# A page of output weights in two transfers, and a gate and an output sum put in another order, in a two-layer decode kernel on Trainium2

## The chip, the cores and the metric

The kernel runs on one core of a Trainium2 chip. The engines are named as in the profile: PE (TensorE, matrix products; PEld is its weight load), DVE (VectorE), ACT (ScalarE), POOL (GpSimd) and SP (SyncE, which here issues nearly all transfers). A core has 16 DMA engines. The metric is the device time of one execution in microseconds (us), as the median of several executions. The profile comes from one further execution.

## The reference

One token goes through two identical layers, each an attention over a cached window and then a gated feed-forward block. The caches and the weights are the same in both layers.

```python
def _A_ref(x, k_cache, v_cache, wq, wo):
    # x: (1, 1, 640); 32 heads of 192; window W = 4096 of 32768 cached positions
    q = (x @ wq).reshape(1, 1, 32, 192) ...
    k = k_cache[:, :, Sk - W:, :]
    v = v_cache[:, :, Sk - W:, :]
    scores = einsum("bhqd,bhkd->bhqk", q, k) * (192 ** -0.5)
    o = einsum("bhqk,bhkd->bhqd", softmax(scores), v)
    return o.reshape(1, 1, 6144) @ wo

def _B_ref(x, w1, w3, w2):            # 640 -> 1536 -> 640
    return (silu(x @ w1) * (x @ w3)) @ w2

x = A_x
x = x + _A_ref(_layernorm(x), ...)
x = x + _B_ref(_layernorm(x), ...)
x = x + _A_ref(_layernorm(x), ...)
x = x + _B_ref(_layernorm(x), ...)
```

All inputs are bf16. Some 1.5 MB for each head's K window, as much for its V window, 7.9 MB each for wq and wo and 5.9 MB for w1, w2 and w3 make the work one of moving data: every weight meets a single vector.

## The kernel before

**Pages and the queue.** SBUF holds an arena of 16 slots of 12,288 bytes per partition. A list, `loads`, names every page in the order in which it is wanted: for each layer five pages of wq, the K and V windows head by head (V trails K by six heads), six pages of wo, and four of the feed-forward block. These four are `fa` (most of w1), `fb` (most of w3), `fc` (the rest of w1, the rest of w3 and four of the twelve row chunks of w2, three transfers) and `fd` (five more chunks of w2). The last three chunks of w2 stay in SBUF in `keep` from layer 0, and the last three chunks of wo in `wo5`. `refill` (line 200) issues transfers from SP as long as a slot is free; `done` frees a slot and calls `refill`. So the order of transfers is fixed by the list, and their time by free slots. There is one further limit: the framework gives the transfers eight completion semaphores in turn, so that a transfer is issued only when the one eight places ahead has landed. Fourteen heads' K pages (`RETAIN`) are kept from layer 0 and not loaded again in layer 1.

A transfer covers all 128 partitions. Each of the 16 DMA engines moves eight of the rows and reports on its own, and a transfer counts as landed when all 16 have.

**The end of a layer.** Everything that the change touches lies behind the last V page, most of it in the last 20 us.

- `wo_proj` (line 397) multiplies the 48 chunks of the attention's output with wo, page by page in the order 0 to 5. Page 4 (`("o", 1, 4)`, nine chunks, one transfer of 1440 KB in layer 1) is the last that arrives; page 5 is `wo5`. Each chunk is two matmuls of 128x320, spread over four column groups of PE.
- `y_to_residual` (line 245) copies the sums to SBUF on ACT (L247) and DVE (L248), turns them with five small matmuls, and adds them to the residual `xsq` (L252).
- `layernorm` (line 229) squares (L230), sums over partitions with one fp32 matmul, and works out the mean and the scale on DVE and ACT (L234 to L242). It writes `xs`.
- `ffn` (line 417) multiplies `xs` with the pages: g with `fa`, u with `fb`, then the last quarter-rows of g and u with `fc`. g is copied out by ACT (L444), u by DVE (L445). Three small matmuls each turn g and u into the partition layout, both into the same bank `m_ps`. Then come exp(-g) on ACT (L451), a copy of u (L454), g*u (L456), 1+exp (L458), its reciprocal (L459) and the product (L460), which gives `htd`, the twelve columns of the block's hidden vector.
- In layer 0, `y_open` (line 390) zeroes two PSUM tiles with two matmuls and 24 matmuls multiply `htd` with w2.
- In layer 1, `last_rows` (line 477) forms the output. At the start of `ffn`, POOL has spread the residual x over a matrix `xw` and built an identity in a free slot (L422 to L429). `last_rows` adds x through five fp32 matmuls with `xw` (ten instructions, as fp32 goes in two passes), then the 48 matmuls of w2's chunks in the order 0 to 3, 9 to 11, 4 to 8. Chunk 8 is the last transfer of the kernel, 160 KB. DVE copies the row (L489) and SP sends it out (L491).

PE, DVE and ACT each run their instructions in the program's order.

Of the kernel before, what the change touches and what calls it, by code (L numbers as in the profile page):

```python
# [15 lines left out]
P = 128  # L16
D = 640
NCH = 5
# [29 lines left out]
def kernel(  # L48
# [79 lines left out]
    ptm = cst.tile([P, 16 * PW], BF16, name="ptm")  # L128
    otd = cst.tile([P, 48], BF16, name="otd")
    htd = cst.tile([P, 12], BF16, name="htd")  # L130
    zero = cst.tile([P, 32], BF16, name="zero")
    nc.gpsimd.memset(zero[:], 0.0)
    w20 = cst.tile([P, 768], BF16, name="w20")
    qt_sb = cst.tile([P, H, 6], BF16, name="qt_sb")
# [28 lines left out]
    for layer in range(2):  # L163
        for c in range(NCH):
            loads.append((("q", layer, c), [(0, PGW, wq_v[c])]))
        for i in range(H + LEAD):
            for kind, g, cache in (("v", i - LEAD, A_v_cache), ("k", i, A_k_cache)):
                if not 0 <= g < H:
                    continue
                h = head(layer, g)  # L170
                if kind == "k" and layer == 1 and h in RETAIN:
                    if h == STASH:
                        loads.append((("k", 1, h), []))
                    continue
                loads.append(((kind, layer, h),
                              [(0, PGW, cache[0, h, S0:SK, :].rearrange("(p t) d -> p (t d)", p=P))]))
        for w in range(6):
            parts = []
            for at, ci in enumerate(wo_order(layer)[9 * w:9 * w + 9]):
                blk, e = ORDER[layer][ci // 12], ci % 12  # L180
                if parts and parts[-1][2] == blk and parts[-1][3] + parts[-1][1] == e:
                    parts[-1][1] += 1
                else:
                    parts.append([at, 1, blk, e])
            parts = [(640 * at, 640 * n, wo_v[blk][:, 640 * e:640 * (e + n)]) for at, n, blk, e in parts]
            if w < 5:
                loads.append((("o", layer, w), parts))
            elif layer == 0:
                assert len(parts) == 1 and parts[0][1] == 1920
                loads.append((None, [(wo5[:], parts[0][2])]))  # L190
        loads.append((("fa", layer), [(0, PGW, w1_v[:, 0:PGW])]))
        loads.append((("fb", layer), [(0, PGW, w3_v[:, 0:PGW])]))
        loads.append((("fc", layer), [(0, 1536, w1_v[:, PGW:]), (1536, 1536, w3_v[:, PGW:]),
                                      (3072, 2560, w2_v[:, 0:2560])]))
        fd = [(0, 3200)] if layer == 0 else [(0, 1280), (1280, 1280), (2560, 640)]
        loads.append((("fd", layer), [(o, n, w2_v[:, 2560 + o:2560 + o + n]) for o, n in fd]))
        if layer == 0:
            loads.append((None, [(keep[:], w2_v[:, 5760:7680])]))
# [197 lines left out]

    def wo_proj(layer):
        y_ps = y_open("y_ps")
        for w in range(6):
            pg = page(("o", layer, w)) if w < 5 else wo5  # L400
            for cc, ci in enumerate(wo_order(layer)[9 * w:9 * w + 9]):
                n = 9 * w + cc
                j = n % 4
                for nh in range(2):
                    mm(y_ps[nh][32 * j:32 * j + 1, 0:320], lhsT=otd[:, ci:ci + 1],
                       rhs=pg[:, 640 * cc + 320 * nh:640 * cc + 320 * nh + 320],
                       start=False, stop=(n >= 44), tile_position=(0, 32 * j))
            if w < 5:
                done(("o", layer, w))
        y_to_residual(y_ps)  # L410
# [6 lines left out]
    def ffn(layer):  # L417
        if layer == 1:
            assert not loads
            spare = free[0] * PGW  # L420
            ident = arena[:, spare:spare + 64].bitcast(F32)
            nc.gpsimd.memset(ident, 0.0)  # L422
            for j in range(4):
                nc.gpsimd.affine_select(out=ident, in_=ident, compare_op=ALU.not_equal, fill=1.0, base=-32 * j,
                                        pattern=[[-1, 32]], channel_multiplier=1)
            xw = arena[:, spare + 64:spare + 64 + 1280].bitcast(F32)
            nc.gpsimd.memset(xw, 0.0)
            for j in range(4):
                nc.gpsimd.tensor_copy(out=xw[32 * j:32 * j + 32, 32 * j:640:128], in_=xsq[32 * j:32 * j + 32, 0:NCH])  # L429
            ident = (ident, xw)  # L430
        g_ps = ps_a.tile([P, 512], F32, tag="a", name="g_ps")
        u_ps = ps_a.tile([P, 512], F32, tag="a", name="u_ps")
        for ps, kind, c0, c1, off in ((g_ps, "fa", 0, 4, 0), (u_ps, "fb", 0, 4, 0),
                                      (g_ps, "fc", 4, 5, 0), (u_ps, "fc", 4, 5, 1536)):
            pg = page((kind, layer))
            for c in range(c0, c1):
                for j in range(4):
                    mm(ps[32 * j:32 * j + 32, 0:384], lhsT=xs[:, c, 3:35],
                       rhs=_ap(pg, 0, P, off + 1536 * (c - c0) + 3 * j, [[12, 128], [1, 3]]),
                       start=(c == 0), stop=(c == NCH - 1), tile_position=(0, 32 * j))  # L440
            if kind != "fc":
                done((kind, layer))
        gu = w20.rearrange("p (g n) -> p g n", g=2)
        pin(nc.scalar.copy(out=gu[:, 0, :], in_=g_ps[:, 0:384]))  # L444
        pin(nc.vector.tensor_copy(out=gu[:, 1, :], in_=u_ps[:, 0:384]))  # L445
        gt_ps = m_ps[:, 0:24].rearrange("p (g k j) -> p g k j", g=2, k=3)
        for gi in range(2):
            for k in range(3):
                mm(gt_ps[:, gi, k, :], lhsT=gu[:, gi, k:384:3], rhs=sel4[:], start=True, stop=True)
        ex = sml.tile([P, 12], F32, tag="ex", name="ex")  # L450
        pin(nc.scalar.activation(out=ex[:], in_=gt_ps[:, 0, :, :].rearrange("p k j -> p (k j)"), func=ACTF.Exp,  # L451
                                 scale=-1.0))
        ut = sml.tile([P, 12], F32, tag="ut", name="ut")
        pin(nc.vector.tensor_copy(out=ut[:], in_=gt_ps[:, 1, :, :].rearrange("p k j -> p (k j)")))  # L454
        gut = sml.tile([P, 12], F32, tag="gut", name="gut")
        pin(nc.vector.tensor_tensor(out=gut[:], in0=gt_ps[:, 0, :, :].rearrange("p k j -> p (k j)"), in1=ut[:],  # L456
                                    op=ALU.mult))
        pin(nc.vector.tensor_scalar_add(out=ex[:], in0=ex[:], scalar1=1.0))  # L458
        pin(nc.vector.reciprocal(out=ex[:], in_=ex[:]))  # L459
        pin(nc.vector.tensor_tensor(out=_ap(htd[:], 0, P, 0, [[1, 3], [3, 4]]),  # L460
                                    in0=gut[:].rearrange("p (k j) -> p k j", k=3),
                                    in1=ex[:].rearrange("p (k j) -> p k j", k=3), op=ALU.mult))
        if layer == 1:
            return last_rows(ident)
        y_ps = y_open("y2_ps")
        for fcx in range(12):
            j = fcx % 4
            pg, off = w2_chunk(layer, fcx)
            for nh in range(2):
                mm(y_ps[nh][32 * j:32 * j + 1, 0:320], lhsT=htd[:, fcx:fcx + 1], rhs=pg[:, off + 320 * nh:off + 320 * nh + 320],  # L470
                   start=False, stop=(fcx >= 8), tile_position=(0, 32 * j))
            if fcx == 3:
                done(("fc", layer))
        done(("fd", layer))
        y_to_residual(y_ps)

    def last_rows(ident):
        f_ps = ps_a.tile([P, 512], F32, tag="a", name="f_ps")
        eye, xw = ident
        for c in range(NCH):  # L480
            mm(f_ps[:, c:160:NCH], lhsT=xw[:, 128 * c:128 * c + 128], rhs=eye, start=(c == 0), stop=False)
        for fcx in (0, 1, 2, 3, 9, 10, 11, 4, 5, 6, 7, 8):
            pg, off = w2_chunk(1, fcx)
            for j in range(4):
                mm(f_ps[32 * j:32 * j + 1, 0:160], lhsT=htd[:, fcx:fcx + 1],
                   rhs=pg[:, off + 160 * j:off + 160 * j + 160],
                   start=False, stop=(fcx == 8), tile_position=(0, 32 * j))
        row = w20[:, 0:160]
        pin(nc.vector.tensor_copy(out=row, in_=f_ps[:, 0:160]))  # L489
        ps = row.ap[0][0]  # L490
        nc.sync.dma_start(out=out[0, 0, :].rearrange("(j i) -> j i", j=4),  # L491
                          in_=bass.AP(row.tensor, row.offset, [[32 * ps, 4], [1, 160]]))
# [69 lines left out]
```

## Time and profile before

| | |
|---|---|
| time before, median of 3 | 528.51 us (528.39 to 528.86) |
| profiled execution, its own time | 528.32 us |
| its span, first to last instruction | 526.6 us |
| read from HBM | 221.58 MB |
| busy: PE, DVE, ACT, POOL | 275.0, 256.4, 62.5, 16.2 us |
| transfers issued on SP: median time to landing, K and V pages | 29.2 us |
| transfers of wo, 1440 / 960 / 480 KB: median time to landing | 15.3 / 16.8 / 21.8 us |
| DMA rate in 40 slices, second to second last | 419 to 433 GB/s |

The profiled execution's time is 1.7 us above its span, for what lies before the first and behind the last instruction. In the page, a line such as "PE MATMUL f_ps<-arena,htd 128*1 128x160 bf16 x36" is a group of 36 matmuls that read the tiles arena and htd and write f_ps, with one column of weights and 160 columns streamed. An arrow in brackets behind a row names what ended the engine's idle time before it. "DMA to landing" is the time from the issue of a transfer on SP until all 16 DMA engines have reported. The PE clock is given as the share that was granted, 0.5 or 1.0.

### The profile page before, as it was taken

What the parts mean: (1) busy time and instruction counts of PE and PEld (TensorE: products, weight loads), DVE (VectorE), ACT (ScalarE), POOL (GpSimd) and SP (SyncE); (2) the same over time, 40 slices, a digit from 0 to 9 for tenths busy, and PEclk for the clock granted to TensorE, in tenths of its full rate; (3) what the DMA queues carried; (4) which work ended last, traced back from release to release, by engine and by line L of the source; (5) the groups of instructions that cost most, each with busy time, mean ns of one, the idle gap of its engine ahead of it and who ended that gap; (6) DMA issues with size and microseconds to landing.
All of it is one profiled execution on the core that took longest, in us unless ns stands there. A gap on an engine that the chain in (4) does not pass through costs nothing.

```text
span 526.6 us, 5978 instructions
## 1 busy us (share of the span) xinstructions
PE 275.0 (52%) x2403; PEld 112.6 (21%) x2403; DVE 256.4 (49%) x393; ACT 62.5 (12%) x192; POOL 16.2 (3%) x74
## 2 busy tenths in 40 slices
PE   2344644472655644455545555687254756345455
PEld 1111211131222221122112112233022322112113
DVE  1199676556657475654002139531475645753001
ACT  1002020110102020112001002022111120202000
POOL 4000000000000000000000000000000000001000
PEclk9997968666756776586556558988677886686557
DMA  8999999999999999999999999999999999999995
GB/s 349 429 430 433 426 428 427 433 432 427 427 428 432 432 426 429 428 432 423 419 431 422 427 428 427 420 431 427 428 428 431 429 428 429 429 431 428 424 432 242
DMA packets 22355, 221.97 MB, mean 421 GB/s; under 512 B 2616, under 2 KB 2744, under 8 KB 5176
## 3 DMA queue, kind: packets, MB, share of 16 engines
q1 hardware_dynamic: 22184, 221.59, 99.3%
q8 instruction: 19, 0.31, 0.2%
q14 instruction: 8, 0.07, 0.0%
q10 hardware_dynamic: 144, 0.00, 0.0%
HBM read 221.58 MB, written 0.00 MB: 421 GB/s over the span
## 4 chain that ended last, share of the span: by engine, by line
DMA 85%; PE 7%; DVE 5%; issue 1%; ACT 1%; SPq 1%; DVEq 0%; ACTq 0%
DMA arena<-in_A_k_cache_dram 51%; DMA arena<-in_A_v_cache_dram 16%; DMA arena<-in_A_wo_dram 9%; DMA arena<-in_B_w_dram 6%; DMA arena<-in_A_wq_dram 3%; DVE arena L300 3%; PE s_ps L80 3%; PE o_ps L80 2%; PE y_ps L80 1%; SPq L210 1%; PE q_ps L80 1%; PE u_ps L80 0%; PE pss L80 0%; ACT w L337 0%; DVE t L322 0%
## 5 line engine op out<-in xcount | busy, mean ns | idle before, releaser
L80 PE MATMUL s_ps<-arena,wst 128*32 128x512 bf16 x768 | 153.7, 512 | 171.3 <-DVE arena L300 84.5
L300 DVE STREAM_TRANSPOSE arena<-arena 128x1536 uint32<-128x1536 uint32 x100 | 171.2, 1754 | 75.0 <-DMA arena<-in_A_k_cache_dram 74.6
L80 PE MATMUL o_ps<-arena,ptm 128*8 128x384 bf16 (+1 forms) x1024 | 113.5, 421 | 12.9 <-DMA arena<-in_A_v_cache_dram 12.9
L80 PEld LDWEIGHTS <-wst 128*32 128x32 bf16 x768 | 53.1, 115 | 256.2 <-issue 227.1
L80 PEld LDWEIGHTS <-ptm 128*8 128x8 bf16 (+1 forms) x1024 | 40.0, 99 | 49.9 <-issue 40.3
L332 ACT ACTIVATE tb<-m 32x16 f32<-32x16 f32 x16 | 3.4, 214 | 280.4 <-DVE m L329 280.4
L350 ACT COPY ptm<-w 32x64 bf16<-32x64 bf16 x80 | 23.6, 295 | 42.5 <-PE o_ps L80 39.3
L80 PE MATMUL y_ps<-arena,otd 128*1 128x320 bf16 x180 | 16.9, 459 | 15.1 <-DMA arena<-in_A_wo_dram 15.1
L80 PE MATMUL q_ps<-arena,xs 128*32 128x512 bf16 x120 | 14.5, 624 | 17.3 <-DMA arena<-in_A_wq_dram 14.7
L383 DVE SCALAR_TENSOR_TENSOR w<-pss,rl,mask 64x192 bf16<-64x192 f32 x16 | 6.7, 417 | 32.2 <-PE pss L80 32.2
L282 POOL COPY wst<-qt_sb 32x24 bf16<-32x24 bf16 x30 | 8.4, 281 | 432.7 <-PE s_ps L80 313.8
L340 DVE STREAM_TRANSPOSE w<-w 64x512 bf16<-64x512 bf16 x16 | 11.3, 705 | 14.4 <-ACT w L337 14.4
L248 DVE CAST w<-y_ps 128x320 bf16<-128x320 f32 x3 | 1.5, 490 | 34.4 <-PE y_ps L80 34.4
L322 DVE TENSOR_REDUCE t<-s_ps 64x1 f32<-64x512 f32 x16 | 10.6, 663 | 12.2 <-PE s_ps L80 12.1
L274 DVE CAST qt_sb<-pss 32x192 bf16<-32x192 f32 x2 | 0.7, 346 | 31.2 <-PE pss L80 31.2
L350 DVE COPY ptm<-w 32x64 bf16<-32x64 bf16 x48 | 9.9, 207 | 10.8 <-PE o_ps L80 9.6
L80 PEld LDWEIGHTS <-xs 128*32 128x32 bf16 x200 | 7.2, 119 | 35.7 <-issue 26.1
L355 DVE RECIPROCAL rl<-pss 64x1 f32<-64x1 f32 x16 | 2.6, 166 | 22.2 <-PE pss L80 22.2
L80 PEld LDWEIGHTS <-otd 128*1 128x1 bf16 x192 | 6.4, 103 | 25.8 <-issue 21.7
L337 ACT ACTIVATE w<-s_ps,nbt 64x512 bf16<-64x512 f32 x16 | 10.9, 682 | 5.6 <-DVE nbt L334 5.6
L376 ACT CAST w<-o_ps 128x384 bf16<-128x384 f32 x16 | 7.7, 479 | 33.0 <-PE o_ps L80 23.7
L80 PE MATMUL pss<-w,sel 128*64 128x192 bf16 x32 | 6.3, 286 | 9.5 <-ACT w L376 6.4
(82 smaller groups left out, 111.8 us busy)
## 6 DMA issues: line engine op xcount, KB each, us to landing
arena<-in_A_v_cache_dram SPq DMA_DIRECT2D x64, 1536.0 KB, 29.2
arena<-in_A_k_cache_dram SPq DMA_DIRECT2D x50, 1536.0 KB, 29.2
arena<-in_A_wq_dram SPq DMA_DIRECT2D x10, 1536.0 KB, 9.3
arena<-in_A_wo_dram SPq DMA_DIRECT2D x6, 1440.0 KB, 15.3
arena<-in_B_w_dram SPq DMA_DIRECT2D x4, 1536.0 KB, 11.1
arena<-in_A_wo_dram SPq DMA_DIRECT2D x4, 960.0 KB, 16.8
arena<-in_A_wo_dram SPq DMA_DIRECT2D x4, 480.0 KB, 21.8
arena<-in_B_w_dram SPq DMA_DIRECT2D x4, 384.0 KB, 14.6
```

Source lines behind the costliest of these rows:

```text
L80: return pin(nc.tensor.matmul(*a, **k))
L210: pin(nc.sync.dma_start(out=arena[:, s * PGW + off:s * PGW + off + n], in_=src))
L282: pin((engs[a].copy if engs[a] is nc.scalar else engs[a].tensor_copy)(out=dst, in_=src))
L300: pin(nc.vector.transpose(x[:, w * sp:w * (sp + 1)].bitcast(U32), x[:, w * sp:w * (sp + 1)].bitcast(U32)))
L322: pin(nc.vector.reduce_max(out=t0[:, 0:1], in_=s_ps[0:64, :], axis=AX.X))
L332: pin(nc.scalar.mul(out=tb[32:64, :].rearrange("p (a z) -> p a z", a=4)[:, :, 0:HB], in_=mb, mul=-SCALE))
L337: pin(nc.scalar.activation(out=e[:], in_=s_ps[0:64, :], func=ACTF.Exp, bias=nbt[:, 0:1], scale=SCALE, accum_out=l[:]))
L340: pin(nc.vector.transpose(et[:], e[:]))
L350: pin((eng.copy if eng is nc.scalar else eng.tensor_copy)(out=dst, in_=src))
L355: pin(nc.vector.reciprocal(out=rl[half], in_=rl_ps[half]))
L376: pin(nc.scalar.copy(out=o_sb[:, 0:384], in_=o_ps[:, 0:384]))
L383: pin(nc.vector.scalar_tensor_tensor(out=om, in0=ot_ps[half], scalar=rl[half], in1=mask[half].unsqueeze(2).broadcast_to([64, 16, 12]), op0 ...
```

## The change

1. In layer 1, wo's page 4 is loaded in two transfers into the same slot: its first six chunks (960 KB) and its last three (480 KB).
2. In layer 1, `wo_proj` takes the three kept chunks of `wo5` ahead of page 4 and not behind it.
3. The x term of the output is added earlier: the five fp32 matmuls stand at the start of `ffn`, behind layernorm's sum on PE and ahead of g's first matmul. They go to the first columns of the tile `pss` and not to a rotating bank.
4. The gate is split. In both layers g alone is copied, turned and passed through exp, 1+exp, reciprocal and the product g/(1+exp(-g)), while u is copied and turned after it. u's three turning matmuls write to unused columns of g's own bank, and the last product reads u from there. The copy of u to SBUF (L454) and one tile (`gut`) are gone.
5. In `last_rows`, the kept chunks 9 to 11 go first, then 0 to 8.
6. The tile `zero` is 64 columns wide and not 32. The removal of `gut` takes 64 bytes out of each partition of SBUF, the wider `zero` adds 64, and the arena keeps its address.

In the built program the count of PE instructions is the same, DVE has two operations less, and SP issues one transfer more.

```diff
@@ loads, wo's pages
+            if layer == 1 and w == 4:
+                (at, n, blk, e), = parts
+                parts = [[at, n - 3, blk, e], [at + n - 3, 3, blk, e + n - 3]]
@@ def wo_proj(layer):
-        for w in range(6):
+        for w in (0, 1, 2, 3, 4, 5) if layer == 0 else (0, 1, 2, 3, 5, 4):
             pg = page(("o", layer, w)) if w < 5 else wo5
...
@@ def ffn(layer):
-            ident = (ident, xw)
+            f_ps = pss[:, 0:160]
+            for c in range(NCH):
+                mm(f_ps[:, c:160:NCH], lhsT=xw[:, 128 * c:128 * c + 128], rhs=ident, start=(c == 0), stop=False)
         g_ps = ps_a.tile([P, 512], F32, tag="a", name="g_ps")
         u_ps = ps_a.tile([P, 512], F32, tag="a", name="u_ps")
+        gu = w20.rearrange("p (g n) -> p g n", g=2)
+        gt_ps = (m_ps[:, 0:12], g_ps[:, 384:396])
...
+        def turn(gi):
+            for k in range(3):
+                mm(gt_ps[gi][:, 4 * k:4 * k + 4], lhsT=gu[:, gi, k:384:3], rhs=sel4[:], start=True, stop=True)
+
+        def gate():
+            pin(nc.scalar.copy(out=gu[:, 0, :], in_=g_ps[:, 0:384]))
+            turn(0)
+            pin(nc.scalar.activation(out=ex[:], in_=gt_ps[0], func=ACTF.Exp, scale=-1.0))
+            pin(nc.vector.tensor_scalar_add(out=ex[:], in0=ex[:], scalar1=1.0))
+            pin(nc.vector.reciprocal(out=ex[:], in_=ex[:]))
+            pin(nc.vector.tensor_tensor(out=ut[:], in0=gt_ps[0], in1=ex[:], op=ALU.mult))
...
         pin(nc.vector.tensor_copy(out=gu[:, 1, :], in_=u_ps[:, 0:384]))
-        gt_ps = m_ps[:, 0:24].rearrange("p (g k j) -> p g k j", g=2, k=3)
-        for gi in range(2):
-            ...
-        pin(nc.vector.tensor_copy(out=ut[:], in_=gt_ps[:, 1, :, :].rearrange("p k j -> p (k j)")))
-        ...
+        gate()
+        turn(1)
         pin(nc.vector.tensor_tensor(out=_ap(htd[:], 0, P, 0, [[1, 3], [3, 4]]),
-                                    in0=gut[:].rearrange("p (k j) -> p k j", k=3),
-                                    in1=ex[:].rearrange("p (k j) -> p k j", k=3), op=ALU.mult))
+                                    in0=gt_ps[1].rearrange("p (k j) -> p k j", k=3),
+                                    in1=ut[:].rearrange("p (k j) -> p k j", k=3), op=ALU.mult))
@@ def last_rows(f_ps):
-        f_ps = ps_a.tile([P, 512], F32, tag="a", name="f_ps")
-        eye, xw = ident
-        for c in range(NCH):
-            mm(f_ps[:, c:160:NCH], lhsT=xw[:, 128 * c:128 * c + 128], rhs=eye, start=(c == 0), stop=False)
-        for fcx in (0, 1, 2, 3, 9, 10, 11, 4, 5, 6, 7, 8):
+        for fcx in (9, 10, 11, 0, 1, 2, 3, 4, 5, 6, 7, 8):
```

More of the change, by code (lines that the diff above doesn't have):

```diff
@@ L130 @@
     htd = cst.tile([P, 12], BF16, name="htd")
-    zero = cst.tile([P, 32], BF16, name="zero")
+    zero = cst.tile([P, 64], BF16, name="zero")
     nc.gpsimd.memset(zero[:], 0.0)
@@ L398, in wo_proj @@
         y_ps = y_open("y_ps")
-        for w in range(6):
+        for w in (0, 1, 2, 3, 4, 5) if layer == 0 else (0, 1, 2, 3, 5, 4):
             pg = page(("o", layer, w)) if w < 5 else wo5
             for cc, ci in enumerate(wo_order(layer)[9 * w:9 * w + 9]):
-                n = 9 * w + cc
+                n = 9 * w + cc if w < 4 or layer == 0 else cc + (36 if w == 5 else 39)
                 j = n % 4
@@ L429, in ffn @@
                 nc.gpsimd.tensor_copy(out=xw[32 * j:32 * j + 32, 32 * j:640:128], in_=xsq[32 * j:32 * j + 32, 0:NCH])
-            ident = (ident, xw)
+            f_ps = pss[:, 0:160]
+            for c in range(NCH):
+                mm(f_ps[:, c:160:NCH], lhsT=xw[:, 128 * c:128 * c + 128], rhs=ident, start=(c == 0), stop=False)
         g_ps = ps_a.tile([P, 512], F32, tag="a", name="g_ps")
         u_ps = ps_a.tile([P, 512], F32, tag="a", name="u_ps")
+        gu = w20.rearrange("p (g n) -> p g n", g=2)
+        gt_ps = (m_ps[:, 0:12], g_ps[:, 384:396])
+        ex = sml.tile([P, 12], F32, tag="ex", name="ex")
+        ut = sml.tile([P, 12], F32, tag="ut", name="ut")
+        def turn(gi):
[8 more added lines that the diff above has]
+            pin(nc.vector.tensor_tensor(out=ut[:], in0=gt_ps[0], in1=ex[:], op=ALU.mult))
         for ps, kind, c0, c1, off in ((g_ps, "fa", 0, 4, 0), (u_ps, "fb", 0, 4, 0),
@@ L442, in ffn @@
                 done((kind, layer))
-        gu = w20.rearrange("p (g n) -> p g n", g=2)
-        pin(nc.scalar.copy(out=gu[:, 0, :], in_=g_ps[:, 0:384]))
         pin(nc.vector.tensor_copy(out=gu[:, 1, :], in_=u_ps[:, 0:384]))
-        gt_ps = m_ps[:, 0:24].rearrange("p (g k j) -> p g k j", g=2, k=3)
-        for gi in range(2):
[L448 to L453, printed above, removed]
-        pin(nc.vector.tensor_copy(out=ut[:], in_=gt_ps[:, 1, :, :].rearrange("p k j -> p (k j)")))
[L455 to L459, printed above, removed]
+        gate()
+        turn(1)
         pin(nc.vector.tensor_tensor(out=_ap(htd[:], 0, P, 0, [[1, 3], [3, 4]]),
-                                    in0=gut[:].rearrange("p (k j) -> p k j", k=3),
-                                    in1=ex[:].rearrange("p (k j) -> p k j", k=3), op=ALU.mult))
+                                    in0=gt_ps[1].rearrange("p (k j) -> p k j", k=3),
+                                    in1=ut[:].rearrange("p (k j) -> p k j", k=3), op=ALU.mult))
         if layer == 1:
-            return last_rows(ident)
+            return last_rows(f_ps)
         y_ps = y_open("y2_ps")
@@ L475, in ffn, with last_rows @@
         y_to_residual(y_ps)
-    def last_rows(ident):
-        f_ps = ps_a.tile([P, 512], F32, tag="a", name="f_ps")
-        eye, xw = ident
-        for c in range(NCH):
-            mm(f_ps[:, c:160:NCH], lhsT=xw[:, 128 * c:128 * c + 128], rhs=eye, start=(c == 0), stop=False)
-        for fcx in (0, 1, 2, 3, 9, 10, 11, 4, 5, 6, 7, 8):
+    def last_rows(f_ps):
+        for fcx in (9, 10, 11, 0, 1, 2, 3, 4, 5, 6, 7, 8):
             pg, off = w2_chunk(1, fcx)
```

## The prediction

> **What bounds the kernel now.** I read the page first, for what fills the span; then the chain of waits of the last 45 us; then the timeline, the transfers' rows and the windows of the last 10 us, where nearly all of the change lies.
>
> From the page, the transfers of the main queue and the chain by engine:
>
> ```profile
> q1 hardware_dynamic: 22184, 221.59, 99.3%
> DMA 85%; PE 7%; DVE 5%; issue 1%; ACT 1%; SPq 1%; DVEq 0%; ACTq 0%
> ```
>
> The 16 DMA engines move data for 99.3% of the span, and 85% of the chain is transfers. The time is that of the bytes, plus what follows the last of them. The chain's end (start, length, what):
>
> ```profile
> 467.07 29.51 DMA arena<-in_A_wo_dram
> ...
> 496.64 21.04 DMA arena<-in_B_w_dram
> ...
> 517.72 1.21 PE u_ps L80 x10
> ...
> 520.14 0.57 DVE w L445
> ...
> 522.23 1.16 PE f_ps L80 x48
> 523.39 0.02 issue
> 523.41 0.32 DVE w L489
> ```
>
> By this view, 5.7 us of computing stand between the landing of `fb` (496.64 + 21.04 = 517.68) and the output copy. The reader should not stop here: the 48 matmuls are drawn as one block. The timeline of their last pieces and then the rows of SP's last load, w2's chunk 8, show that the block has a wait inside:
>
> ```profile
> 522.92 0.44 PE L80 MATMUL f_ps<-arena,htd 128*1 128x160 bf16 x8
> 523.12 0.24 PE L80 MATMUL f_ps<-arena,htd 128*1 128x160 bf16 x4
> ```
>
> ```profile
> L210 SPq DMA_DIRECT2D arena<-in_B_w_dram x1: 327/327/327, 510.4 to 510.4; - x1
> ...
> DMA to landing us min/median/max: 12.7/12.7/12.7
> ```
>
> Chunk 8 is issued at 510.4 and lands 12.7 later, at 523.1 (523.08 in the trace's completion records). The four matmuls that need it start at 523.12. Chunks follow each other every 0.07 us, the four before began at 522.92, so these could have started at 522.99 and waited 0.13. The kernel already ends with its last transfer. The windows agree: the DMA engines are full until 520 and run out until 523.
>
> ```profile
> 519.00:520.00 1.00, 1.00 (x10) 0.10 (x3) 0.00 (x0) 0.29 (x1) 0.00 (x0) 1.00 0.99 397
> 520.00:521.00 1.00, 0.57 (x10) 0.41 (x8) 0.56 (x1) 0.19 (x1) 0.00 (x0) 1.00 0.71 279
> 521.00:522.00 1.00, 1.00 (x10) 1.00 (x10) 0.66 (x5) 0.18 (x1) 0.00 (x0) 1.00 0.48 183
> 522.00:523.00 1.00, 0.90 (x46) 0.79 (x46) 0.18 (x1) 0.00 (x0) 0.00 (x0) 1.00 0.11 42
> ```
>
> (The last three columns are the granted clock, the DMA share and GB/s.) They run out slowly because the engines are not level: chunk 8's sixteen reports come from 519.94 to 523.08.
>
> **Part by part, in the order of the work.**
>
> *Page 4 in two transfers.* No byte is saved; one more transfer is queued on SP. Its price is what each DMA engine pays for eight more rows and one more report. In the packet records a row of 11,520 bytes takes 432 ns, one of 7,680 takes 291 and one of 3,840 takes 149: 8 ns more, times eight rows, is 0.064 us; a report is 9 ns. The completion records give the same from outside: from one landing to the next, wo's 1440 KB took 3.42 us, and 480 and 960 KB together 1.14 + 2.28 = 3.42 on one page and 2.29 + 1.21 = 3.50 on the other. So 0 to 0.08; I take 0.06, nearest to the rows' sum. A gain is excluded, since the engines are busy throughout. All of it reaches the end, since everything behind it in the queue is later by it.
>
> One thing is moved past nothing but shifts: the transfer eight places ahead, which each issue waits for. With one more transfer, `fa` and all that follow wait for a later landing; `fb` goes out at about 497.7, not 496.64, and the first 320 KB of `fd` at 506.9, not 503.6. What hides that is the queue: at 510.4, before chunk 8's issue, the trace has 4.3 MB issued and not moved, 10 us at 430 GB/s, and chunk 8 is issued off page 4's last landing as before. Were that cover gone, an issue would show up one for one. On SP only the output's transfer stands behind.
>
> *wo5 first, and the split.* Before, 24 matmuls stood behind page 4's landing (489.6 + 20.7 = 510.3), and the copies to SBUF began at 512.27. They go in fours every 0.27 us with 0.47 for the last: six need 0.27 + 0.47 + 0.11 to the copy, 0.85, not 1.89. So residual and layernorm come 1.0 us earlier, `xs` at 514.6 and not 515.6. What is late next is `fb`, at 517.68: the chain above starts there and nothing before it counts. Nothing is gained.
>
> *The x term behind layernorm's sums.* Ten fp32 instructions move from under the gate to ahead of g on PE. At clock 1.0 they took 1.27 us; here the clock is 0.5, so 2.54. They wait for POOL's spreading, which ended at 514.47 and now ends at 513.5, so they end at 516.0. Behind them in PE's order is g, which could have started at 514.6 and before started at 515.64. g's sixteen matmuls with `fa` go in fours every 0.32 us, 1.3 in all: 517.3. `fb` lands at 517.74. The cover is 0.4 us; beyond it every tenth goes into the chain. Price: 0. At the other end of the chain they free nothing, since the ten ran while DVE worked (until 522.13, `htd` until 522.18).
>
> *g's half first, u in g's bank.* Unchanged up to the copy of u, which begins at 520.14 (+0.06) and takes 0.57: it waits for the last quarter of w3, landed at 519.52. Meanwhile g is copied, turned and through exp, by about 520.8. Behind u's copy DVE has 1+exp, reciprocal and two products, by the starts of the old rows 0.20 + 0.26 + 0.20 + 0.24 = 0.90: `htd` is usable at 521.70. Before it was 522.23 (+0.06). 0.59 us earlier.
>
> *Where these 0.59 go.* Kept chunks first: 521.70 to 521.91; chunks 0 to 3 (landed 521.1) to 522.19; 4 and 5 (522.0) to 522.33; then 6 and 7 wait for 522.77, and chunk 8 for 523.14. A wait of 0.44 and one of 0.2 take the place of the computing. The last four matmuls start at 523.18. Gain 0.
>
> *Layer 0's gate.* y_open's two zeroing matmuls (0.43) now stand behind `htd`, as u's turned half lies in the bank that they reuse; `htd` is 0.6 earlier there too. Before, the ninth matmul of w2 waited 0.31 for `fd`, which ends this stage again. Price 0. Hidden by: a transfer, and behind that a queue that never ran dry on the latest engine (its landings stay 3.6 us apart through 285 to 335).
>
> *zero and gut.* One memset of 32 columns more on POOL, in the first microseconds, beside wq's first page. 0.
>
> Sum: +0.06. The profiled execution's 528.32 becomes 528.38. The median was 0.19 above that execution, so I predict 528.51 + 0.06 = 528.57, say 528.6. 0.2% is 1.06 us, about what a measurement of this kernel can tell from no change; this is far within.
>
> **Rivals.**
>
> A. *The gain arrives.* If in the timed runs the last reports come 0.5 us sooner than in the profiled one, the computing is what ends, and of 0.59 some 0.5 stay: 528.0. For it: the spread of 3.1 us between engines is the sum of chance-like instruction fetches (19 packets of 16 KB, 0.9 us each; at 481.8 us one put 0.64 on the last landing). Against: the fetches hang on the program, and the runs differ by 0.5 in all. More than 0.6 cannot come this way.
>
> B. *PE at half clock to the end.* Before, the clock rose to 1.0 at 518.1 and held over the last matmuls. It follows PE's own activity, which the change moves. Half clock alone: 12 chunks at 0.137 put chunk 8 at 523.2, and 0.2 more for its latency: 528.8. If the x term's instructions also don't overlap (0.39 each, as layernorm's fp32 pass takes, 3.9 in all), u starts at 518.7 (513.5 + 3.9 + 1.3), `htd` comes at 522.4, chunk 8 at 523.9, the copy 0.9 later than before: 529.4. For it: 37 us at 0.5 before 518.1. Against: the windows behind were granted 1.0 on 1.95 us of PE work in 3.41.
> The Trainium skill, "TensorE: Matmul & The Clock Gate", Part 1, says that the clock is released after about 3.4 us of sustained activity, in a free-running window. The trace has stretches of 3.41 us, and a half-busy one sufficed.
>
> C. *The new transfer costs a fixed time.* Place: on each DMA engine, between page 4's two parts. A transfer alone, the output's, takes from 523.80 to 525.45, 1.65 us, for 1.2 KB. Were that paid in the queue, all behind it is 1.65 later: 530.2. It decides above 1.06 us. Against: the pairs of wo above, 0 to 0.08.
> The Trainium skill, "DMA: Bandwidth & Descriptors", section "Anatomy of one DMA", gives some 2.0 us fixed per transfer, for POOL's path; by that, 530.5. It puts most of it down to the wait for the write's receipt; here it overlaps the next transfer, as the landings show.
>
> D. *A fetch falls on the last engine:* +0.6, 529.2; on another, at most −0.11, the gap to the second last report. SP's stream is longer and DVE's shorter; PE's, with most fetches, is as long as before.
>
> **Numbers.** Forecast 0.75, A 0.08, B 0.07, D 0.03: together 0.93 within 0.2%. C 0.03 and something unseen 0.02 are slower by more; 0.02 unseen is faster. The range, 528.1 to 529.2, holds the runs' own spread, D and most of B, and leaves C and the best of A out.
>
> **What the next profile would show.** Right: page 4 as 960 and 480 KB, the second landing at 510.4; `xs` near 514.6 and then PE idle or in the x term before `fb`; `htd` near 521.7; a wait on a transfer ahead of chunks 6 and 8; the last four matmuls at 523.2 and the output copy at 523.5. Wrong: u's first matmul later than 517.8 (the x term in the way), clock 0.5 behind 518, or a last landing off by more than 0.3 from 523.1.

## The result, and the profile after

The changed kernel takes 529.66 us in the median (529.07 to 530.73, 18 runs); the kernel before, measured beside it, 528.65 us (528.34 to 529.59, 18 runs). The ratio is 1.0016, with a 95% interval of 1.0009 to 1.0022: 0.85 us slower by the ratio, with an interval of 0.5 to 1.2 us (the two medians are 1.01 apart). The forecast was 528.6, no change, in a range that ended at 529.2; it was reckoned from a first measurement of the kernel before, 528.51, 0.14 under the one beside the changed kernel. The profiled execution took 529.12 us (528.32 before), its span 527.3 us (526.6 before).

First the end of the chain of waits of the changed kernel (start, length, what). It answers to the chain shown of before:

```profile
493.27 17.22 DMA arena<-in_A_wo_dram
...
510.55 12.60 DMA arena<-in_B_w_dram
523.15 0.04 issue
523.20 0.27 PE pss L80 x4
523.46 0.02 issue
523.49 0.33 DVE w L493
```

The gate has left the chain. It goes straight from w2's chunk 8, landed at 510.55 + 12.60 = 523.15, to the four matmuls that need it and the output copy. The copy starts at 523.49, and before at 523.41. Up to here the whole change has cost 0.08 us. The timeline of the same stretch shows the moved work:

```profile
513.60 1.53 PE L80 MATMUL pss<-arena 128*128 128x32 f32 x10 [0.41 <-POOL arena L432]
...
514.16 0.30 DVE L245 TENSOR_SCALAR xs<-xsq,st,rstd 128x5 bf16<-128x5 f32 x1 [0.51 <-ACT rstd L244]
515.06 1.55 PE L80 MATMUL g_ps<-arena,xs 128*32 128x384 bf16 x16
517.85 1.57 PE L80 MATMUL u_ps<-arena,xs 128*32 128x384 bf16 x16 [1.24 <-DMA arena<-in_B_w_dram]
...
520.24 0.56 DVE L465 CAST w<-u_ps 128x384 bf16<-128x384 f32 x1 [5.79 <-PE u_ps L80]
...
521.65 0.19 DVE L468 TENSOR_TENSOR htd<-g_ps,ut 128x12 bf16<-128x12 f32 x1
521.89 0.38 PE L80 MATMUL pss<-keep,htd 128*1 128x160 bf16 x12 [0.79 <-DVE htd L468]
522.10 1.34 PE L80 MATMUL pss<-arena,htd 128*1 128x160 bf16 x36
523.49 0.33 DVE L493 CAST w<-pss 128x160 bf16<-128x160 f32 x1 [1.65 <-PE pss L80]
523.88 0.65 SPq L495 DMA_DIRECT2D out_dram<-w  x1
```

The x term, layernorm and g are done well before u's page lands, and `htd` is used at 521.89, 0.34 us earlier than before. The 36 matmuls that read the arena then spread over 1.34 us, because they wait for transfers: two of w2's loads land at 522.75 and 523.15, and the matmuls that need them start at 522.79 and 523.20. So far the prediction holds, and the kernel should be 0.08 us slower. The other 0.8 us lie behind the last line, where the chain ends. The waits of SP in the last microseconds show them (what waited, for what, total, times, longest). Before:

```profile
SPq L557 <- DMA out_dram<-w: 1.0, 1, 1.0
```

After:

```profile
SPq L561 <- DMA out_dram<-w: 1.7, 1, 1.7
```

SP waits 0.7 us longer for the landing of the output, 1.2 KB in four rows. From its issue to its last report it took 523.80 to 525.46 before, 1.66 us, and 523.88 to 526.32 now, 2.44 us. The transfer is the same. What is new stands in the page's list of queues (packets, MB, share); before:

```profile
q8 instruction: 19, 0.31, 0.2%
q14 instruction: 8, 0.07, 0.0%
```

After:

```profile
q8 instruction: 19, 0.31, 0.2%
q14 instruction: 9, 0.07, 0.0%
```

Within the span there is one more packet of instructions. In the packet records it is 8 KB, starts at 524.98 and takes 0.40 us. In the trace of before the same packet stands at 527.25, behind the span. Three of the output's four rows start at 525.13 to 525.16, and the fourth at 525.37, where the 8 KB packet ends. Three of the four reports come at 525.51 to 525.53, 0.38 us behind their rows, as all four did before (0.36); the fourth comes at 526.32, 0.95 behind its row. So some 0.2 us are lost at the row and 0.57 at its report. PE's last packet of 16 KB lies near by in both kernels (523.23 to 524.16 before, 523.01 to 524.03 now), but it ends before the output's rows start.

The Trainium skill, "DMA: Bandwidth & Descriptors", section "Queues, rings and completion order", says that a DMA engine takes packets from its queues in turn, and that the report of a transfer is written only after every earlier write of that engine, across its queues. The late row agrees with the first: it starts as the 8 KB packet ends. The late report would follow from the second if the fetch's own write was confirmed that late, which no run here measures by itself.

### The profile page after: what moved, and what is told of

Its sections match the earlier page's. It is cut to its first block, busy times and chain, and to the rows that moved or that the text cites. A ratio compares the mean times of both kernels' runs of the same rounds, so it can differ in the third digit from the quotient of the medians.

```text
span 527.3 us, 5982 instructions
## 1 busy us (share of the span) xinstructions
PE 277.7 (53%) x2403; PEld 113.0 (21%) x2403; DVE 256.2 (49%) x391; ACT 62.5 (12%) x192; POOL 16.3 (3%) x74
## 4 chain that ended last, share of the span: by engine, by line
DMA 86%; PE 6%; DVE 5%; issue 1%; ACT 1%; SPq 1%; DVEq 0%; ACTq 0%
DMA arena<-in_A_k_cache_dram 57%; DMA arena<-in_A_v_cache_dram 14%; DMA arena<-in_A_wo_dram 7%; DMA arena<-in_B_w_dram 4%; DVE arena L303 4%; DMA arena<-in_A_wq_dram 3%; PE s_ps L80 3%; PE o_ps L80 1%; PE y_ps L80 1%; SPq L213 1%; PE q_ps L80 1%; PE pss L80 0%; ACT w L340 0%; DVE t L325 0%; ACT wst L285 0%
## 5 line engine op out<-in xcount | busy, mean ns | idle before, releaser
L80 PE MATMUL o_ps<-arena,ptm 128*8 128x384 bf16 (+1 forms) x1024 | 116.5, 426 | 12.4 <-DMA arena<-in_A_v_cache_dram 12.4
```

What stands on the lines that cost most here:

```text
L80: return pin(nc.tensor.matmul(*a, **k))
```

## The experiments

**The theories.** Theory I: DVE's instruction stream is two instructions longer, which pulls its last refill from behind the kernel's end into the output's landing. The operations on DVE are two fewer, 391 and not 393. But two of the new ones wait for two engines at once, in each layer, and the second wait is an instruction of its own. These are their rows in the changed kernel (groups of one source line each):

```profile
L453 DVEq EVENT_SEMAPHORE  x2: 21/21/21, 287.6 to 521.3; - x2
```

```profile
L468 DVEq EVENT_SEMAPHORE  x2: 21/21/21, 287.8 to 521.6; - x2
```

Four instructions more and two less: in the trace DVE's stream has 450 records and not 448. Theory S, the rival: the split of page 4 makes SP's stream two longer, 297 and not 295, and the refill is SP's. What speaks for I ahead of any run: in both traces the packet starts 1.1 us after the end of DVE's 447th record, which is the closing drain behind the output copy now (523.87), and the second drain of the closing barrier before (526.15).

**1. The changed kernel without the split.**

```diff
-            if layer == 1 and w == 4:
-                (at, n, blk, e), = parts
-                parts = [[at, n - 3, blk, e], [at + n - 3, 3, blk, e + n - 3]]
```

> The changed kernel with wo's page 4 in one transfer again; all else of the change is kept. Theory I (DVE's instruction stream is two instructions longer, so that a fetch of 8 KB of instructions falls on the output's transfer): DVE is as long as in the changed kernel, so the fetch stays at about 525.0 us and the output's landing takes 2.4 us and not 1.7; 0.7 to 0.8 us slower than the kernel before, 0.06 faster than the changed one. Theory S (SP's stream, two instructions longer through the split, sets the fetch off): the fetch goes back behind the end (527 us), the time is that of the kernel before, within 0.1 us.

Measured: ratio 1.0023 (1.0014 to 1.0032), 1.2 us slower than before. The packet comes at 526.36, 1.1 us after the drain, in an execution that ran 1.4 us later as a whole (its output copy starts at 524.87 for 523.49). SP waits as long as with the split:

```profile
SPq L558 <- DMA out_dram<-w: 1.8, 1, 1.8
```

Theory S falls. The loss stays without the split; it is somewhat more than the 0.7 to 0.8 expected, and the interval reaches down to 0.74.

**2. The split alone in the kernel before.** The same three lines, added to the kernel before.

> The kernel before with wo's page 4 in two transfers and nothing else; SP's stream is two instructions longer, DVE's is unchanged. Theory I: the fetch stays behind the end at about 527 us, and only the split's own price is left, 0.06 us slower than before. Theory S: fetch at about 525 us, 0.85 us slower.

Measured: ratio 1.0002 (0.9992 to 1.0012). The packet stays at 527.36, and the wait for the output is the old one:

```profile
SPq L560 <- DMA out_dram<-w: 0.9, 1, 0.9
```

**3. Two more instructions on DVE in the kernel before, and nothing of the change.**

```diff
     nc.vector.memset(onesb[:], 1.0)
+    nc.vector.memset(onesb[:], 1.0)
+    nc.vector.memset(onesb[:], 1.0)
```

> The kernel before with the initial memset of one small constant on DVE made three times and not once; it happens in the first microseconds beside the first load, and no part of the change is in. Theory I: DVE's stream is as long as in the changed kernel, the fetch of 8 KB comes at about 525 us, the output lands 0.8 us later, 0.7 to 0.8 us slower than before. Theory S and every theory that blames a part of the change: no difference, within 0.1 us.

Measured: ratio 1.0017 (1.0008 to 1.0026), 0.9 us slower. The page and the waits have both signs:

```profile
q14 instruction: 9, 0.07, 0.0%
```

```profile
SPq L559 <- DMA out_dram<-w: 1.8, 1, 1.8
```

Two memsets in the first microseconds, beside the first load, cost as much as the whole change. This is the run that carries the verdict: none of the change's parts is in it.

**4. The whole change, with DVE's stream as long as before.**

```diff
-    nc.vector.memset(onesD[:], 1.0 / D)
+    nc.gpsimd.memset(onesD[:], 1.0 / D)
-    nc.vector.memset(onesb[:], 1.0)
+    nc.gpsimd.memset(onesb[:], 1.0)
```

> The whole change, with two initial memsets of small constants moved from DVE to POOL, so that DVE's stream is as long as in the kernel before. Theory I: the fetch goes back to 527 us, the output lands in 1.7 us, and the time is 0.06 to 0.1 us above the kernel before. Theory S: as the changed kernel, 0.85 us slower.

Measured: 528.57 us, ratio 0.9998 (0.9989 to 1.0007). The loss is gone, and no gain shows. In its profile:

```profile
q14 instruction: 8, 0.07, 0.0%
```

```profile
SPq L561 <- DMA out_dram<-w: 0.9, 1, 0.9
```

**5 and 6. One instruction more, and forty.** The first is the kernel before with one extra memset, the second the whole change with forty.

> The kernel before with the small initial memset on DVE made twice: DVE's stream is one instruction longer. Theory I, with its point of decision: the fetch followed by 1.1 us the end of the same instruction of DVE's stream, the 447th in the trace, in both profiles. With one instruction more that place is taken by the wait for the closing barrier, which ends at about 526.0, so that the fetch comes at about 527.1, behind the output: no difference from before, within 0.1 us. Rival L (each further instruction costs something of its own, 0.4 us here, half of what two cost): 0.4 us slower.

> The whole change with forty more memsets of the small constant on DVE at the start. Theory I: the same fetch now comes some 40 instructions earlier, in the last tens of us and not at the output, where it only takes one of the 16 DMA engines 0.3 to 0.4 us; the output lands in 1.7 us. 0.06 us above the kernel before if that engine is not the last one, 0.4 above if it is. Rival L (the length of DVE's stream costs by itself): 0.85 us slower than before or more.

Measured: 1.0002 (0.9991 to 1.0013) with one, and 0.9999 (0.9990 to 1.0007) with forty. With one the 447th record is the wait that the expectation named; in an execution 1.2 us later as a whole it ends at 527.25, and the packet comes at 528.58, behind the output. With forty the packet comes at 466.74, in the middle of the stream of loads, and costs nothing that can be measured. Four of the queue's nine packets have moved against the changed kernel: 52.93, 222.02, 366.75 and 524.98 became 15.22, 172.42, 330.11 and 466.74, while the other five stayed within 1 us. So these four are DVE's. The last is the ninth packet of the page's list now, but the output lands as before:

```profile
q14 instruction: 9, 0.07, 0.0%
```

```profile
SPq L601 <- DMA out_dram<-w: 0.9, 1, 0.9
```

So not the length of the stream costs, but where its last refill falls. Rival L falls by the run with forty, where it forecast 0.85 us or more and the interval ends at 0.4. The run with one doesn't decide it: its interval reaches 0.7 us and still holds the 0.4 that L forecast there.

The trace's records put the six runs and the two kernels in one table (us from the start of each span):

| kernel | end of DVE's 447th record | packet starts | wait for the output |
|---|---|---|---|
| before | 526.15 | 527.25 | 1.0 |
| the change | 523.87 | 524.98 | 1.7 |
| change without the split | 525.25 | 526.36 | 1.8 |
| before with the split | 526.22 | 527.36 | 0.9 |
| before, 2 more | 523.93 | 525.06 | 1.8 |
| change, 2 fewer | 526.88 | 527.99 | 0.9 |
| before, 1 more | 527.25 | 528.58 | 1.0 |
| change, 40 more | 463.29 | 466.74 | 0.9 |

**7 and 8. Is the gate's gain real?** The gate's shorter chain ran into the wait for w2's last transfers. To see it by itself, the transfers are taken out of its way: in both kernels layer 1's last five chunks of w2 are loaded ahead of the gate's weights.

```diff
-        loads.append((("fd", layer), [(o, n, w2_v[:, 2560 + o:2560 + o + n]) for o, n in fd]))
+        loads.insert(len(loads) - (3 if layer else 0), (("fd", layer), [(o, n, w2_v[:, 2560 + o:2560 + o + n]) for o, n in fd]))
```

> The kernel before with the loads of layer 1's last five chunks of w2 (800 KB, 1.9 us) moved ahead of the gate's weights. No work is left out. The last transfers are then those that the gate itself waits for, so that all computing of the gate stands behind them: w3's last quarter lands at about 521.4, not 519.5, and the output copy starts 1.9 us later; 1.9 us slower than before.

> The whole change with two memsets moved from DVE to POOL and the same order of loads as in the run just above, so that no transfer stands behind the gate. If the gate's shorter chain is real and was only hidden by w2's last transfers: 0.5 us faster than the run just above (0.59 of the gate less 0.06 of the split), 1.4 us slower than before. If it is not real: as the run just above, or slower by 0.06.

Measured: 1.0051 (1.0036 to 1.0065) and 1.0033 (1.0021 to 1.0046), 2.7 and 1.7 us slower than the kernel before. The difference is 1.0 us in the medians, but the two intervals overlap, so the times alone don't settle it. The profiles are sharper. The timeline of the first, with the old gate:

```profile
523.24 0.56 DVE L445 CAST w<-u_ps 128x384 bf16<-128x384 f32 x1 [6.42 <-PE u_ps L80]
...
525.34 0.45 PE L80 MATMUL f_ps<-arena,htd 128*1 128x160 bf16 x16
...
526.39 0.33 DVE L489 CAST w<-f_ps 128x160 bf16<-128x160 f32 x1 [1.11 <-PE f_ps L80]
```

And of the second, with the new one:

```profile
523.71 0.56 DVE L465 CAST w<-u_ps 128x384 bf16<-128x384 f32 x1 [7.70 <-PE u_ps L80]
...
525.28 0.38 PE L80 MATMUL pss<-keep,htd 128*1 128x160 bf16 x12 [0.72 <-DVE htd L468]
525.49 0.80 PE L80 MATMUL pss<-arena,htd 128*1 128x160 bf16 x36
526.34 0.33 DVE L493 CAST w<-pss 128x160 bf16<-128x160 f32 x1 [1.11 <-PE pss L80]
```

From the start of u's copy to the output's copy the old gate takes 3.15 us and the new one 2.63, both at a granted clock of 1.0. This stretch is 0.5 us shorter when no transfer stands behind the gate. The two profiled executions don't differ by as much (531.31 and 531.18), since the last quarter of w3 landed 0.47 us later in the second (523.10 for 522.63). Why both kernels lost more than expected (2.7 for 1.9 and 1.7 for 1.4, though 1.9 is the lower end of the first interval and 1.4 lies inside the second) is not settled; in the first profile the last page of wo, which lands ahead of the reordered loads, was already 1.2 us later than in the kernel before (511.56 for 510.34).

No version came out faster than the kernel before by more than its interval.

## Why the prediction was wrong

Its steps up to the output copy held, all but the x term's end to 0.2 us:

- *What bounds.* Right. The last transfer ends the kernel, before and after.
- *Page 4 in two transfers.* Predicted +0.06; the last landing moved from 523.08 to 523.15. Alone it can't be told from nothing (run 2). Rival C, a fixed price for the new transfer, falls.
- *wo5 first, and the split.* `xs` was to be ready at 514.6; it was at 514.16 + 0.30 = 514.46. It gained nothing, as said.
- *The queue and layer 0's gate.* `fb` went out at 497.83 for 497.7 and the first part of `fd` at 507.03 for 506.9, hidden as said. The last of layer 0's feed-forward loads landed where it did before (290.56 for 290.55).
- *The x term.* Predicted to end at 516.0 at half clock; g started at 515.06, as most of the ten ran at full clock in this execution (1.53 us for all). At half clock, in run 8, they took 2.31 us where 2.54 was estimated, and nowhere near rival B's 3.9. That g had 1.2 us to spare before `fb`'s landing is in good part luck of the clock. By an estimate from these rows (513.60 + 2.31, and 1.55 for g, where the prediction put 1.3) g would end at 517.5 at half clock throughout, 0.3 ahead of that landing.
- *The gate.* Its matmuls were to start at 521.70 and started at 521.89. The two extra waits of DVE were not in the sum: the two products start 0.33 and 0.27 us behind the step before them, where 0.26 and 0.20 were reckoned.
- *Where the gain goes.* Right: chunks 6 and 8 wait for their transfers (522.79 and 523.20, predicted 522.77 and 523.18), and the output copy came at 523.49 for 523.5. Run 4 shows the gain of the whole change in time: none.
- *Rival B.* PE's clock was in fact 0.5 until 521.35 here, where before it had been 1.0 from 518.1, and it cost nothing, since PE was not what ended. The reading that a half-busy stretch suffices for 1.0 did not hold. Before, a stretch with 1.95 us of PE work (514.70 to 518.11) was followed by 1.0; now one with 2.17 us was followed by 0.5. The windows of after, cut where the clock changes (PE's busy time is the second number behind each stretch, the first its length, the last three columns are clock, DMA share and GB/s):

```profile
514.52:517.93 3.41, 2.17 (x24) 1.00 (x27) 0.00 (x0) 0.00 (x0) 0.00 (x0) 0.50 0.99 409
517.93:521.35 3.42, 2.75 (x30) 1.17 (x30) 0.96 (x3) 0.66 (x2) 0.00 (x0) 0.50 0.83 332
521.35:524.76 3.41, 1.34 (x48) 0.87 (x48) 0.68 (x3) 0.00 (x0) 0.00 (x0) 1.00 0.15 53
```

Two of the signs that the prediction named for being wrong came true, and neither points at the loss. u's first matmul came at 517.85, behind the 517.8 named, since `fb` landed at 517.80 and not since the x term stood in the way. And the clock was 0.5 behind 518.

**The step that failed** is the one that closed the sum: "Sum: +0.06", with everything behind the output copy taken as it was. The output's landing was treated as a constant, 1.66 us in the trace of before, and it measured 2.44. The 0.08 up to the output's issue and these 0.78 make 0.86 us by the last report. At the end of the span 0.73 of it is left, since what follows the last report took 0.13 us less; the own times of the two profiled executions are 0.80 apart. That fits the 0.85 measured, whose interval is wider than these differences. What the runs showed in its place is DVE's last refill: its 8 KB fall on the output's landing, and two instructions more or less on DVE bring the loss (run 3) or take it away (run 4).

The prediction had the mechanism in hand, as rival D: a fetch of instructions that falls on the wrong engine at the wrong time. But it looked for it ahead of the last load only, among the streams of PE and SP, and set DVE aside with "DVE's shorter". That count was of operations. The waits that stand as instructions of their own were left out, and with them the stream is two longer. So D got 0.03. The trace of before showed an 8 KB packet at 527.25, 1.1 us behind an instruction of DVE's closing barrier, and the change put that place ahead of a wait of more than 2 us. A count of each stream against the place of its last refill would have made D a likely case, though that trace alone doesn't name the engine whose packet it is.

What stays open: why the last refill follows the 447th record. Earlier refills don't keep to a fixed count: the packet that comes at 222.13 in the kernel before, when 193 of DVE's records have ended, came at 197.69 in run 3, when 178 had. Open too is why the report was 0.95 us behind its row where the other three took 0.38. A wait for the fetch's own write would fit that, and so would what is seen behind DVE's other refills (last section), but it was not measured by itself.

## What to carry to other kernels

Where the chain ended in a transfer, work that was saved ahead of its landing was worth nothing: look inside a block of matmuls for the wait, and find the transfer that ends it, before pricing anything else.

Count the instructions of each engine, the waits that stand alone among them, and look at where its last refill falls. The last refill, when it fell into the stream of loads, cost nothing that could be measured (run 6); the same 8 KB beside the last, small transfer cost 0.8 us, and two instructions decided it. Moving two constants to another engine, or forty idle instructions, took the loss away. A profile has to show where the refill falls, as its place could not be told from a count alone.

A kernel doesn't end with its last instruction of work. The output's landing is part of the time, and two profiles that agree up to the output copy can still differ behind it.

## What the runs showed of the hardware

The profile lists the fetches of instructions among the packets of the 16 DMA engines that also move the data: packets of 16 KB on one queue (19 in the span, most of them 0.88 to 0.97 us; they are taken for PE's, whose stream is by far the longest) and of 8 KB on another (0.31 to 0.43 us). DVE's last refill started 1.1 us after the 447th record in six of the table's eight kernels; it was 1.3 in the one with one instruction more, and 3.45 in the one where it fell into the stream of loads.

A refill takes more from its DMA engine than its own time. As each 8 KB packet in the stream of loads ends, a row of data starts that takes longer than the usual 0.46 us for 12 KB. Behind DVE's, at 52.58, 222.13 and 366.81 before and at all four places with forty instructions more, the row takes 0.99 to 1.00 us; behind the other five it takes 0.68 to 0.74. So one refill of DVE's costs one of the 16 DMA engines 0.31 + 0.53 = 0.84 us, about what it cost at the output (some 0.2 at the row and 0.57 at the report), and more than the 0.3 to 0.4 that the expectation of run 6 put on it. In the stream of loads this reaches the end only if that engine is the last one.

The transfers are not level over the 16 engines. The first and the last report of a transfer are 0.3 to 0.5 us apart at the start and 2.8 to 3.6 at the end, over all kernels. In the kernel before, the five steps above 0.6 us in this distance (0.63 to 1.38) each come 2.6 to 4.2 us after one of the 16 KB packets starts (33.3, 257.2, 283.4, 335.8 and 481.8); the other fourteen packets make no such step. The last load's reports there come from 519.94 to 523.08, with a mean of 521.57. By that mean, evening them out would be worth 1.5 us, an estimate, and more than all that this change tried. It was not tried here, since the trace doesn't tell which engine a packet is on.
